# The first chunk of a Conformer block: rows and weights over two DMA queues, layer norm on VectorE, feed-forward matmuls tile by tile

## The chip, the cores and the metric

One core of one Trainium2 chip. The metric is the device time of one execution in microseconds (us); lower is better.

Engines: PE is TensorE (PEld its weight loads), DVE is VectorE, ACT is ScalarE, POOL is GpSimd, SP is SyncE, which only issues transfers here. "L506 PE MATMUL" is a matmul recorded at line 506 of the kernel.

## The reference, cut to what matters

```python
def reference(x, w_ff1_a, w_ff1_b, ...):       # x: 2 x 4000 x 512, bf16
    h = _layernorm(x, axis=-1)
    h = _silu(h @ w_ff1_a) @ w_ff1_b           # 512 -> 2048 -> 512
    x1 = x + 0.5 * h
    ...                                        # attention, convolution, a second feed-forward, layer norm
```

Tokens go through in 16 chunks of four tiles of 127. All that follows is about the first chunk's layer norm and the first four of its 16 feed-forward blocks (128 columns of `w_ff1_a` each). Weights and rows must arrive, be normalised and transposed before PE has real work: this is the head of the program.

## The kernel before

```python
# class Sync: every buffer remembers who wrote and read it; op() and dma() emit the waits
def dma(self, e, dkey, *fns, reads=(), writes=()):
    ...                                        # waits on engine e
    for fn in fns:
        fn(self.eng[e]).then_inc(self.sem[dkey], 16)
    ...

ROWS = ((0, 112), (112, TILE))                 # a tile of 127 rows is loaded in two pieces

def load_rows(self, dst, src, writes, eng):
    k = self.S.dsems[self.nxt("ld", 16)]
    return self.S.dma(eng, k, *[lambda e, lo=lo, hi=hi: e.dma_start(dst[lo:hi], src[lo:hi])
                                 for lo, hi in self.ROWS], writes=writes)

def ln_tiles(self, c, sl, prepare=None, engs=("ACT", "ACT", "ACT", "DVE"), src=None, lag=2):
    def finish(ti):
        if engs[ti] == "ACT":                  # -mean * factor, for ACT's scale and bias
            S.op("DVE", lambda e: e.scalar_tensor_tensor(out=self.sh[sl][:, ti:ti + 1], ...))
        self.ln_norm(c, sl, ti, self.ltm[ti][0:TILE, :], self.b_ltm[ti], engs[ti], src)
    for ti in range(TPC):
        ...
        self.ln_stats(c, sl, ti, src)          # bn_stats, DVE
        if ti >= lag:
            finish(ti - lag)
            yield ti - lag
        if lag == 1 or ti == TPC - 1:
            self.ln_mean(sl, ti)               # bn_aggr, DVE
            self.ln_factor(sl, ti)             # (var + eps) ** -0.5, POOL
    for ti in range(TPC - lag, TPC):
        finish(ti)
        yield ti

def head(self):
    self.warm(14)                              # 508-wide matmuls on zeros
    self.rings["ln"] = 1
    self.early = [self.sbank() for _ in range(4)]   # all four banks of the ring

    def blocks(lo, hi):                        # first layer, blocks 0 to 3, of tiles lo to hi - 1
        for f, (ps, b_ps) in enumerate(self.early):
            out = ps[:, lo * TILE:hi * TILE].rearrange("p (t k) -> p t k", t=hi - lo)
            for cc in range(DC):
                self.mm(out, self.Wa[:, cc, f * 128:(f + 1) * 128], self.lnT[0][:, lo:hi, cc, 0:TILE],
                        cc == 0, cc == DC - 1, [self.b_Wa[f * self.NWA // FC]] + self.b_lnT[0][lo:hi], b_ps)

    for ti in self.ln_tiles(0, 0, lag=1):
        if ti:                                 # four PE transposes, then a copy by ACT
            self.transpose_pe(ti - 1, 0, "ACT", (self.Yb[ti - 1], self.b_Y[ti - 1]))
        if ti == 2:
            blocks(0, 1)
    blocks(1, 2)
    self.transpose_pe(TPC - 1, 0, "DVE", (self.Yb[TPC - 1], self.b_Y[TPC - 1]))
    blocks(2, 4)

def program(self, any_score):
    ...
    for ti in range(TPC):
        self.load_rows(self.XT[ti], ..., [self.bx[ti]], "ACT" if ti == 1 else "SP")
    for k in range(self.NWA):                  # eight pieces of 256 KB of each weight
        self.load_wa(i["w_ff1_a"], k, "SP")
        self.load_wb(i["w_ff1_b"], 2 * k, 2 * k + 2)
        if k == 3:
            self.load_x(1)
    if not any_score:
        self.constants()                       # memsets on DVE and POOL
    self.act(self.nr1, self.onef, AF.Silu, ...)     # loads ACT's table early
    self.head()
    ...
```

`Wa0` and `Wa1` are the first two pieces of `w_ff1_a`: they hold blocks 0 to 3. `Wb0` is the first piece of `w_ff1_b`. After the head come the activations of the four early blocks and block 4, which uses the PSUM bank of block 0 again.

Of the kernel before, what the change touches and what calls it, by code (L numbers as in the profile page):

```python
# [15 lines left out]
TILE = 127  # L16
TPC = 4
# [10 lines left out]
DC = D // 128  # L28
FC = F // 128
# [51 lines left out]
class Sync:  # L81
# [103 lines left out]
        return None  # L185

    def dma(self, e, dkey, *fns, reads=(), writes=()):
        req = self._required(reads, writes)
        prev = self.count[dkey]
        if prev > 0:  # L190
            v = req.get(dkey)
            if v is None or v.val < prev:
                req[dkey] = Ev(dkey, prev, {})
        self._emit_waits(e, req)
        for fn in fns:
            fn(self.eng[e]).then_inc(self.sem[dkey], 16)
            self.count[dkey] += 16
        ev = Ev(dkey, self.count[dkey], dict(self.clock[e]))
        self._bind(ev, reads, writes)
        return ev  # L200

# [45 lines left out]
class Conformer:  # L247
# [315 lines left out]
        k = self.S.dsems[16 + self.nxt("tr", 12)]  # L563
        return self.S.dma("SP", k, lambda e: e.dma_start_transpose(dst, src), reads=reads, writes=writes)

    def load_rows(self, dst, src, writes, eng):
        k = self.S.dsems[self.nxt("ld", 16)]
        return self.S.dma(eng, k, *[lambda e, lo=lo, hi=hi: e.dma_start(dst[lo:hi], src[lo:hi])  # L568
                                     for lo, hi in self.ROWS], writes=writes)

    def store(self, dst, src, reads, writes):
        k = self.S.dsems[36 + self.nxt("st", 8)]
# [126 lines left out]

    def head(self):  # L700

        self.warm(14)
        self.rings["ln"] = 1
        self.early = [self.sbank() for _ in range(4)]

        def blocks(lo, hi):
            for f, (ps, b_ps) in enumerate(self.early):
                out = ps[:, lo * TILE:hi * TILE].rearrange("p (t k) -> p t k", t=hi - lo)
                for cc in range(DC):
                    self.mm(out, self.Wa[:, cc, f * 128:(f + 1) * 128], self.lnT[0][:, lo:hi, cc, 0:TILE],  # L710
                            cc == 0, cc == DC - 1, [self.b_Wa[f * self.NWA // FC]] + self.b_lnT[0][lo:hi], b_ps)

        for ti in self.ln_tiles(0, 0, lag=1):
            if ti:
                self.transpose_pe(ti - 1, 0, "ACT", (self.Yb[ti - 1], self.b_Y[ti - 1]))
            if ti == 2:
                blocks(0, 1)
        blocks(1, 2)
        self.transpose_pe(TPC - 1, 0, "DVE", (self.Yb[TPC - 1], self.b_Y[TPC - 1]))
        blocks(2, 4)  # L720

    def ln_mean(self, sl, ti):
        self.S.op("DVE", lambda e: e.bn_aggr(self.mv[sl][:, ti, :], self.st[sl][:, ti, :]),
# [616 lines left out]
    def program(self, any_score):  # L1340
        i = self.i
# [4 lines left out]
        self.scr = self.OT.rearrange("p c k -> p (c k)")[:, 0:512]  # L1346

        for ti in range(TPC):
            self.load_rows(self.XT[ti], self.x_flat[ti * TILE:(ti + 1) * TILE, :], [self.bx[ti]], "ACT" if ti == 1 else "SP")
        for k in range(self.NWA):  # L1350
            self.load_wa(i["w_ff1_a"], k, "SP")
            self.load_wb(i["w_ff1_b"], 2 * k, 2 * k + 2)
            if k == 3:
                self.load_x(1)
# [129 lines left out]
        for jj in range(DC):  # L1484
# [9 lines left out]
            else:  # L1494
                f, copy = self.depthwise(tail - 1, DC - 1)
# [131 lines left out]
```

## Time and profile before

| | before |
|---|---|
| time, median of the first three runs | 2045.01 us (2044.95 to 2045.12) |
| span of the profiled execution | 2040.1 us |
| PE busy | 2029.2 us, 98% of the chain that ended last |
| block 4 starts (PE runs without a stop after it) | 13.06 us |

The traced execution took 2043.9 us, about 1.1 us less than each of the timed ones, which have no trace.

The prediction reads the page, PE's timeline and the chain of the head. One view is added, VectorE's timeline in the head. Its columns are start, length, engine, line, operation, operands, count, and in brackets the idle time just before and what ended it.

```profile
7.15 0.16 DVE L676 SCALAR_TENSOR_TENSOR work<-work 127x1 f32<-127x1 f32 x1 [0.17 <-POOL work L728]
7.23 0.19 DVE L723 BATCH_NORM_AGGREGATE work<-work 127x2 f32<-127x9 f32 x1
8.15 0.41 DVE L638 TENSOR_SCALAR work<-xt,work 127x512 bf16<-127x512 bf16 x1 [0.74 <-POOL work L728]
```

This is the end of the layer norms: tile 2's shift for ScalarE, tile 3's aggregation, 0.74 us of waiting for GpSimd's power, and the only normalisation that VectorE does itself.

### The profile page before, as it was taken

How to read it: one execution, taken by the hardware profiler on the slowest of the kernel's cores; microseconds unless marked ns; L12 is line 12 of the kernel's file. 1: busy time of each engine (PE TensorE's matmuls, PEld its weight loads, DVE VectorE, ACT ScalarE, POOL GpSimd, SP SyncE). 2: the span in 40 equal slices, each digit the busy share in tenths (PEclk: the TensorE clock that was granted, in tenths of full speed). 3: DMA queues.
4: the chain of work that ended last, by engine and by line, in shares of the span. 5: the costliest groups of instructions: out<-in, count | busy, mean ns of one | idle time of the engine just before them, and what ended most of it. 6: DMA issues, size and time to landing. Idle time of an engine off the chain costs nothing.

```text
span 2040.1 us, 24550 instructions
## 1 busy us (share of the span) xinstructions
PE 2029.2 (99%) x9665; PEld 1029.8 (50%) x9667; DVE 1081.1 (53%) x2187; ACT 746.9 (37%) x1280; POOL 107.7 (5%) x235
## 2 busy tenths in 40 slices
PE   9999999999999999999999999999999999999998
PEld 5555555554444444445444444444455555555555
DVE  4234443334556667666766676667674444434433
ACT  3433333333333333333333333333345443443433
POOL 1000000000000000000000000000011000000000
PEclk9999999999999999999999999999999999999999
DMA  8222245320101111114421111111143111111111
GB/s 185 52 62 62 53 100 126 96 70 8 27 16 26 25 33 26 25 25 95 108 57 23 26 28 33 24 26 26 44 135 93 32 31 42 32 31 42 28 35 38
DMA packets 253122, 104.43 MB, mean 51 GB/s; under 512 B 193412, under 2 KB 252487, under 8 KB 252999
## 3 DMA queue, kind: packets, MB, share of 16 engines
q1 hardware_dynamic: 252751, 102.61, 20.9%
q8 instruction: 78, 1.28, 0.3%
q14 instruction: 45, 0.37, 0.1%
q10 hardware_dynamic: 248, 0.18, 0.0%
HBM read 33.77 MB, written 23.34 MB: 28 GB/s over the span
## 4 chain that ended last, share of the span: by engine, by line
PE 98%; DVE 1%; ACT 0%; DMA 0%; SPq 0%; POOL 0%; issue 0%; DVEq 0%; ACTq 0%
PE s L506 56%; PE y L506 42%; ACT work L556 0%; DVE wff L1206 0%; DMA wff<-in_w_ff_a_dram 0%; SPq L568 0%; POOL work L1215 0%; DVE work L553 0%; DVE wff L1100 0%; PE y L534 0%; ACT keys L556 0%; DVE work L1213 0%; SPq L560 0%; DVE work L869 0%; DVE work L952 0%
## 5 line engine op out<-in xcount | busy, mean ns | idle before, releaser
L556 ACT ACTIVATE work<-s 128x508 bf16<-128x508 f32 (+3 forms) x1060 | 622.7, 588 | 1211.8 <-PE s L506 1208.2
L506 PE MATMUL s<-work,wff 128*128 128x508 bf16 (+5 forms) x2624 | 628.3, 371 | 1.5 <-DVE work L553 0.8
L506 PE MATMUL s<-work,keys 128*128 128x508 bf16 (+1 forms) x2048 | 516.7, 374 | 0.1
L506 PE MATMUL y<-work,keys 128*128 128x508 bf16 (+2 forms) x2048 | 504.2, 373 | 0.4 <-DVE work L553 0.4
L506 PE MATMUL y<-wff,work 128*127 128x512 bf16 (+1 forms) x2000 | 501.4, 378 | 0.0
L952 DVE TENSOR_TENSOR work<-work 128x508 f32<-128x508 f32 (+2 forms) x496 | 334.6, 675 | 282.9 <-ACT work L556 281.8
L506 PEld LDWEIGHTS s<-work,wff 128*128 128x128 bf16 x2624 | 252.3, 98 | 278.0 <-issue 5.0
L506 PEld LDWEIGHTS y<-wff,work 128*127 128x127 bf16 x2000 | 274.4, 137 | 170.8
L506 PEld LDWEIGHTS s<-work,keys 128*128 128x128 bf16 x2048 | 199.4, 98 | 231.9 <-issue 0.6
L506 PEld LDWEIGHTS y<-work,keys 128*128 128x128 bf16 (+1 forms) x2048 | 193.5, 97 | 234.0 <-issue 6.2
L755 DVE SCALAR_TENSOR_TENSOR xt<-y,xt 127x512 bf16<-127x512 f32 x125 | 77.8, 684 | 364.9 <-PE y L506 364.9
L618 DVE BATCH_NORM_STATS2 work<-xt 127x6 f32<-127x512 bf16 x311 | 195.5, 678 | 4.8 <-DMA xt<-in_x_dram 4.7
L506 PE MATMUL s<-work 128*127 128x512 bf16 (+3 forms) x776 | 196.2, 377 | 1.6 <-DVE work L1324 1.2
L625 POOL TENSOR_TENSOR work<-work 127x4 f32<-127x4 f32 (+1 forms) x76 | 76.5, 1007 | 1130.4 <-DVE work L623 1130.4
L506 PEld LDWEIGHTS s<-work 128*127 128x127 bf16 (+1 forms) x776 | 94.7, 124 | 75.7 <-issue 2.7
L638 DVE TENSOR_SCALAR work<-xt,work 127x512 bf16<-127x512 bf16 x306 | 110.4, 407 | 27.0 <-POOL work L625 23.2
L755 DVE SCALAR_TENSOR_TENSOR xt<-s,xt 127x512 bf16<-127x512 f32 x55 | 38.0, 692 | 148.6 <-PE s L506 148.6
L755 DVE SCALAR_TENSOR_TENSOR xt<-s,work,xt 127x512 bf16<-127x512 f32 x64 | 48.0, 750 | 30.8 <-PE s L506 30.2
L1104 DVE SCALAR_TENSOR_TENSOR wff<-wff,s 128x508 bf16<-128x508 f32 (+1 forms) x57 | 38.7, 679 | 41.4 <-PE s L506 41.2
L556 ACT ACTIVATE wff<-s 128x508 f32<-128x508 f32 (+1 forms) x67 | 39.5, 591 | 54.6 <-PE s L506 54.6
L556 ACT ACTIVATE work<-keys,work 128x508 bf16<-128x508 bf16 (+1 forms) x68 | 52.3, 775 | 0.8 <-DVE work L1220 0.7
L1185 POOL COPY wff<-wff 128x1 bf16<-128x1 bf16 x56 | 10.4, 187 | 637.8 <-DVE wff L1104 635.0
(92 smaller groups left out, 415.7 us busy)
## 6 DMA issues: line engine op xcount, KB each, us to landing
keys<-keysd SPq DMA_DIRECT2D x62, 128.0 KB, 2.3
keysd<-work SPq DMA_DIRECT2D x14, 448.0 KB, 3.2
out_dram<-work SPq DMA_DIRECT2D x14, 448.0 KB, 3.2
dcvd<-wff SPq DMA_DIRECT2D x48, 127.0 KB, 1.8
keys<-dcvd SPq DMA_DIRECT2D x12, 508.0 KB, 5.4
xt<-in_x_dram SPq DMA_DIRECT2D x13, 448.0 KB, 4.7
wff<-in_w_ff_a_dram SPq DMA_DIRECT2D x16, 256.0 KB, 5.0
work<-work SPq DMA_TRANSPOSE x208, 2.5
```

Of the source, the lines that this page charges most:

```text
L506: self.S.op("PE", lambda e: e.matmul(out, lhsT, rhs, start=start, stop=stop, **kw), reads=reads, writes=[bank], inc=stop if inc is None el ...
L556: return self.S.op("ACT", lambda e: e.activation(out, in_, func, **kw), reads=reads, writes=writes)
L618: self.S.op("DVE", lambda e: e.bn_stats(self.st[sl][:, ti, 0:6], x), reads=[b_x], writes=[self.b_st[sl][ti]])
L625: S.op("POOL", lambda e: e.tensor_tensor(out=self.rs[sl][:, 0:n], in0=self.mv[sl][:, 0:n, 1], in1=self.neghalf[0:TILE, 0:n], op=ALU.pow), ...
L638: self.S.op("DVE", lambda e: e.tensor_scalar(out, x, self.mv[sl][:, ti, 0:1], self.rs[sl][:, ti:ti + 1], ALU.subtract, ALU.mult), reads=[b ...
L755: self.S.op("DVE", lambda e: e.scalar_tensor_tensor(out=self.XT[g][rows], in0=ps[rows], scalar=scalar, in1=self.XT[g][rows], op0=ALU.mult, ...
L952: S.op("DVE", lambda e, p=p, n=n, acc=acc: e.tensor_tensor(out=acc, in0=acc, in1=self.P[p][0:n, 0:W], op=ALU.add), reads=[self.b_P[p], sel ...
L1104: self.S.op("DVE", lambda e: e.scalar_tensor_tensor(out=out, in0=th, scalar=1.0, in1=ps[:, 0:W], op0=ALU.add, op1=ALU.mult), reads=[b_ps, ...
L1185: S.op("POOL", lambda e: e.tensor_copy(self.G[gs][:, jj, 0:1], self.G[gp][:, jj, CHUNK:CHUNK + 1]), reads=[self.b_G[gp][jj]], writes=[self ...
```

## The change

The intent is to have real work on PE sooner. The small row pieces of tiles 0 and 1, and the first two weights, go out on ScalarE's queue beside SP's; VectorE normalises all four tiles, which leaves ScalarE only the copies of transposes; each tile gets its own matmuls, so that tile 2's hide the copy of tile 3; one warm-up matmul (on zeros, to have PE's clock at its full rate when real work comes) goes.

```diff
@@ head @@
-        self.warm(14)
+        self.warm(13)
...
-        def blocks(lo, hi):
+        def blocks(ti):
             for f, (ps, b_ps) in enumerate(self.early):
-                out = ps[:, lo * TILE:hi * TILE].rearrange("p (t k) -> p t k", t=hi - lo)
                 for cc in range(DC):
-                    self.mm(out, self.Wa[:, cc, f * 128:(f + 1) * 128], self.lnT[0][:, lo:hi, cc, 0:TILE],
-                            cc == 0, cc == DC - 1, [self.b_Wa[f * self.NWA // FC]] + self.b_lnT[0][lo:hi], b_ps)
-
-        for ti in self.ln_tiles(0, 0, lag=1):
+                    self.mm(ps[:, ti * TILE:(ti + 1) * TILE], self.Wa[:, cc, f * 128:(f + 1) * 128],
+                            self.lnT[0][:, ti, cc, 0:TILE], cc == 0, cc == DC - 1,
+                            [self.b_Wa[f * self.NWA // FC], self.b_lnT[0][ti]], b_ps)
+
+        for ti in self.ln_tiles(0, 0, None, ("DVE",) * TPC, lag=1):
+            self.transpose_pe(ti, 0, "DVE" if ti == TPC - 1 else "ACT", (self.Yb[ti], self.b_Y[ti]))
             if ti:
-                self.transpose_pe(ti - 1, 0, "ACT", (self.Yb[ti - 1], self.b_Y[ti - 1]))
-            if ti == 2:
-                blocks(0, 1)
-        blocks(1, 2)
-        self.transpose_pe(TPC - 1, 0, "DVE", (self.Yb[TPC - 1], self.b_Y[TPC - 1]))
-        blocks(2, 4)
+                blocks(ti - 1)
+        blocks(TPC - 1)
@@ program @@
-            self.load_rows(self.XT[ti], ..., [self.bx[ti]], "ACT" if ti == 1 else "SP")
+            self.load_rows(self.XT[ti], ..., [self.bx[ti]], ("SP", "ACT" if ti < 2 else "SP"))
+        for k in range(2):
+            self.load_wa(i["w_ff1_a"], k, "ACT")
         for k in range(self.NWA):
-            self.load_wa(i["w_ff1_a"], k, "SP")
+            if k > 1:
+                self.load_wa(i["w_ff1_a"], k, "SP")
```

(A helper `dma_by` takes one engine for each piece.)

More of the change, by code (lines that the diff above doesn't have):

```diff
@@ L187, in dma, with dma_by @@
     def dma(self, e, dkey, *fns, reads=(), writes=()):
+        return self.dma_by((e,) * len(fns), dkey, *fns, reads=reads, writes=writes)
+    def dma_by(self, engs, dkey, *fns, reads=(), writes=()):
         req = self._required(reads, writes)
@@ L193, in dma @@
                 req[dkey] = Ev(dkey, prev, {})
-        self._emit_waits(e, req)
-        for fn in fns:
+        for e in dict.fromkeys(engs):
+            self._emit_waits(e, req)
+        for e, fn in zip(engs, fns):
             fn(self.eng[e]).then_inc(self.sem[dkey], 16)
             self.count[dkey] += 16
-        ev = Ev(dkey, self.count[dkey], dict(self.clock[e]))
+        snap = dict(self.clock[engs[0]]) if len(set(engs)) == 1 else {}
+        ev = Ev(dkey, self.count[dkey], snap)
         self._bind(ev, reads, writes)
@@ L564, in transpose, with load_rows @@
         return self.S.dma("SP", k, lambda e: e.dma_start_transpose(dst, src), reads=reads, writes=writes)
-    def load_rows(self, dst, src, writes, eng):
+    def load_rows(self, dst, src, writes, engs):
         k = self.S.dsems[self.nxt("ld", 16)]
-        return self.S.dma(eng, k, *[lambda e, lo=lo, hi=hi: e.dma_start(dst[lo:hi], src[lo:hi])
-                                     for lo, hi in self.ROWS], writes=writes)
+        return self.S.dma_by(engs, k, *[lambda e, lo=lo, hi=hi: e.dma_start(dst[lo:hi], src[lo:hi])
+                                                for lo, hi in self.ROWS], writes=writes)
     def store(self, dst, src, reads, writes):
@@ L1348, in program @@
         for ti in range(TPC):
-            self.load_rows(self.XT[ti], self.x_flat[ti * TILE:(ti + 1) * TILE, :], [self.bx[ti]], "ACT" if ti == 1 else "SP")
+            self.load_rows(self.XT[ti], self.x_flat[ti * TILE:(ti + 1) * TILE, :], [self.bx[ti]],
+                           ("SP", "ACT" if ti < 2 else "SP"))
+        for k in range(2):
+            self.load_wa(i["w_ff1_a"], k, "ACT")
         for k in range(self.NWA):
-            self.load_wa(i["w_ff1_a"], k, "SP")
+            if k > 1:
+                self.load_wa(i["w_ff1_a"], k, "SP")
             self.load_wb(i["w_ff1_b"], 2 * k, 2 * k + 2)
```

## The prediction

> **What bounds the kernel now.** I read the page first, then the waits of TensorE (PE) after the first chunk, then the start of the program: the timeline by engine, the chain of waits and the DMA landings.
>
> ```profile
> span 2040.1 us, 24550 instructions
> PE 2029.2 (99%) x9665; PEld 1029.8 (50%) x9667; DVE 1081.1 (53%) x2187; ACT 746.9 (37%) x1280; POOL 107.7 (5%) x235
> ...
> PE 98%; DVE 1%; ACT 0%; DMA 0%; SPq 0%; POOL 0%; issue 0%; DVEq 0%; ACTq 0%
> ```
>
> These are the page's head and its chain by engine. PE is busy for 2029.2 of 2040.1 us and carries 98% of the chain. The longest waits of PE after 39 us sum to 1.6 us (0.4, 0.4 and four of 0.2). So PE works through a fixed list, and any time won before its dense stretch moves everything after it forward by as much. No other stage is touched: set side by side without line numbers, the instruction orders of both kernels differ only in the head (and in its copy in the second, unused branch), but for one load on the SP queue (`w_o`) that now also waits for a weight landed long before. What counts is when PE becomes dense.
>
> The timeline of PE alone, from 5 us (start, length, operation, count, idle time before it and what ended that):
>
> ```profile
> 4.74 1.02 PE L506 MATMUL s<-work 128*128 128x508 bf16 x4
> 6.27 0.40 PE L521 MATMUL y<-work 127*128 127x127 bf16 x4 [0.51 <-ACT work L556]
> 7.21 0.40 PE L521 MATMUL y<-work 127*128 127x127 bf16 x4 [0.54 <-ACT work L556]
> 7.78 0.61 PE L506 MATMUL s<-work,wff 128*128 128x127 bf16 x8 [0.17 <-ACT work L556]
> 8.75 0.62 PE L506 MATMUL s<-work,wff 128*128 128x127 bf16 x8 [0.36 <-DMA wff<-in_w_ff_a_dram]
> 9.21 0.39 PE L521 MATMUL y<-work 127*128 127x127 bf16 x4
> 9.43 1.06 PE L506 MATMUL s<-work,wff 128*128 128x127 bf16 x16
> 10.33 0.39 PE L521 MATMUL y<-work 127*128 127x127 bf16 x4
> 11.33 2.77 PE L506 MATMUL s<-work,wff 128*128 128x254 bf16 x20 [0.61 <-DVE work L553]
> ```
>
> L521 are the transposes of tiles 0 to 3; the x8, x8 and x16 rows are the four first blocks for tile 0 and tile 1; the x20 row is 16 matmuls for tiles 2 and 3 together and 4 of block 4. After the last warm-up matmuls PE waits five times; from 11.33 it never stops. The 254-wide matmuls take about 0.108 us each (half of 0.216, the pitch of a 508-wide one: 4 in 0.866), so **block 4 starts at 11.33 + 16 x 0.108 = 13.06 us**. That moment is my yardstick. The chain over the first 14 us says why it is late:
>
> ```profile
> 3.89 0.51 SPq L560
> 4.40 0.04 issue
> 4.44 4.27 DMA wff<-in_w_ff_a_dram
> 8.71 0.05 issue
> 8.75 0.62 PE s L506 x8
> ```
>
> The second piece of the weights (Wa1) is issued only at 4.44, as the ninth transfer of the SP queue, lands at 8.71, and everything on PE queues behind it.
>
> **What the Trainium skill says.** "DMA: Bandwidth & Descriptors", section "Issuing engines are not separate DMA queues": transfers issued by several engines run on the same 16 DMA engines, and issuing from two saves only sequencer time. The trace has an issue at 0.33 to 0.51 us, so this is what the change can gain: 9 issues in a row on SP end near 4.4. The engines were half busy until 6 us (DMA share 0.50, 149 GB/s) and full from 6 to 8.75 (1.03, 295 GB/s), so issuing earlier does use idle time. "TensorE: Matmul & The Clock Gate", section "What's actually happening": half clock until some 3.4 us of sustained work, and half again after an idle window. The trace agrees with the first half: warm-up matmuls are 0.42 us apart until 4.10 and 0.216 after. "Perfetto Trace Analysis", section "Optimizing Scalar/DVE Operations": an instruction's reported length overlaps the next by its write acknowledgement. The trace agrees: a normalisation on VectorE lasts 0.41, four of them 1.38, so 0.325 each in a row. I use that pitch below.
>
> **The change part by part.**
>
> *Rows over two queues.* Tile 0's 15-row piece was issued at 1.18 and landed 2.3 us later, at 3.48; VectorE began its statistics at 3.47. Issued from ScalarE at 0.73, with the 2.4 us that this queue's pieces took, it lands at 3.13; the other piece at 0.73 + 2.2 = 2.93. VectorE's last memset ends at 3.21. So statistics start near 3.2, a gain of 0.27 us. The other tiles come earlier than needed.
>
> *First weights on ScalarE's queue.* Its two issues took 1.15 us together, so Wa0 goes out near 1.9 and Wa1 near 2.5 (before: 3.44 and 4.44). Wa0 took 2.8 us to land with the engines half busy; Wa1 behind it, sharing with tiles 2 and 3 and then Wb0, I estimate at 4 to 4.5: **6.5 to 7.0 instead of 8.71**. ScalarE's table load (1.28 us) slips to about 3.1 to 4.4, but its first real work comes at 5.8. SP's own weights (Wb1, Wa2, ...) also go out 1.06 us earlier.
>
> *All layer norm on VectorE.* Before, the period per tile was 1.00 us: aggregation at 4.20, power on GpSimd 4.48 to 5.03, a 0.16 us shift at 5.15, next aggregation at 5.22. Now the shift goes and the normalisation (pitch 0.325) stands between the power and the next aggregation. The lag from aggregation to normalisation is 0.92 (7.23 to 8.15 in the trace), so the period is about 0.94 + 0.325 = **1.26 us**. Aggregations: 3.93, 5.20, 6.46, 7.72; normalisations start 4.87, 6.13, 7.39, 8.64 and last 0.41. Tile 3 ends at 9.05, against 8.56 before: this part is slower for the last tile, but tile 0 (ended 6.16 on ScalarE) is now ready at 5.28.
>
> *Order on PE.* 13 warm-ups instead of 14 let go of PE near 5.4. A tile's four transposes occupy 0.22 us (9.21 to 9.43), results out 0.39 after their start; ScalarE's copy lasts 0.58, VectorE's 0.43, each with about 0.14 until PE starts; a tile's 16 matmuls take 0.90 (9.43 to 10.33); a normalisation reaches PE about 0.13 after its end. Step by step: T0 5.41; copy to 6.41. T1 6.67. Block 0 (needs T1 issued, copy 0, weights) 6.89 to 7.79, its Wa1 part at 7.34. T2 7.93; block 1 8.15 to 9.05. T3 9.18; copy on VectorE 9.60 to 10.03. Block 2 9.40 to 10.30 covers that copy, which before cost 0.61 idle. Block 3 10.30 to 11.20. The matmul work itself does not change: 64 x 0.056 = 3.6 against 32 x 0.056 + 16 x 0.108 = 3.5.
>
> *A new wait.* Block 4 uses the PSUM bank of the first early block again, so it needs that one's activation. Its last matmul is now only 12 before block 4: done at 10.30 + 4 x 0.056 + 0.20 = 10.73 (0.20 as 11.76 to 11.96 before), activation 0.59 to 11.32, 0.14 to PE: **block 4 at 11.46**, not 11.20.
>
> Sum: 13.06 - 11.46 = **1.6 us** earlier. After it PE needs Wa2 (before at about 10.3, now about 1 us earlier, needed at 11.46), Wb0 (before 7.0, needed 12.3), Wa3 (12.2, needed 14.9), Wa4 (16.3, needed 19.2): each has a margin, so nothing is given back. The next chunk's rows landed at 15.5 and are used after 37 us.
>
> **The rivals.**
>
> 1. *Weights stay late.* Two queues share the same full engines, and Wb0 may take turns with Wa1. If Wa1 lands at 8.0, its part of block 0 moves from 7.34 to 8.0 and all behind it by at most 0.5: gain 1.1, 2043.9. For: Wa1 took 4.27 in the old order. Against: it had Wa0 and Wb0 ahead of it on one queue, and an engine share of 0.50 before 6 us leaves room.
> 2. *VectorE becomes the bound.* If its period is 1.5 instead of 1.26, tile 3 comes 0.7 later; block 2 hides about 0.1 of it; gain near 1.0, 2044.0. For: normalisation and power now lie in series. Against: each of these durations is from the trace.
> 3. *PE's clock falls back* because one warm-up is gone, or work is thin from 5.4 to 6.7. Then 127-wide matmuls take 0.107 and about 3 us of work doubles: the gain is gone or negative, 2045 to 2047. Against: before, PE had gaps as wide and stayed at full pitch, and the new order is denser by 9 us.
> 4. *More than expected:* no wait for the bank, or PE reached earlier by the chain: at most 0.3 to 0.6 more, 2042.9.
>
> **Range and chances.** 2045.01 - 1.6 = 2043.4; I take 2043.5, as rivals 1 and 2 pull one way. The three times of before lie within 0.17 us, so noise hardly widens it: 2042.7 to 2044.3. Two per cent is 41 us and the whole head is 13, so the verdict must be the same: faster 0.003, same 0.99, slower 0.007.
>
> **What would show it.** Right: statistics of tile 0 near 3.2; normalisations on VectorE 1.26 apart, the last near 8.65; no wait of PE for weights, or below 0.3 us; PE's last idle time a short one (about 0.25) for ScalarE before block 4 near 11.5; the same list after it. Wrong: a weight's DMA in the chain after 7 us; warm-pitch lost (127-wide matmuls 0.1 us apart); block 4 after 12; or, with block 4 early, new DMA waits of PE between 12 and 25 us that give the time back.

## The result, and the profile after

| | before | after |
|---|---|---|
| time, median of four runs | 2045.07 us (2044.95 to 2045.14) | 2043.11 us (2042.81 to 2043.94) |
| span of the profiled execution | 2040.1 us | 2038.9 us |
| block 4 starts in it | 13.06 us | 11.87 us |

A ratio is the mean time of one kernel's fast runs over that of the other's fast runs of the same rounds, so not quite the ratio of the medians. Here it is 0.9991, 95% interval 0.9974 to 1.0008: the same at the 2% level, as forecast, and inside the predicted range (2042.7 to 2044.3).

The head of the page after:

```profile
span 2038.9 us, 24577 instructions
PE 2028.9 (100%) x9682; PEld 1030.0 (51%) x9682; DVE 1081.5 (53%) x2187; ACT 743.7 (36%) x1277; POOL 107.7 (5%) x235
```

PE has as much work as before (2028.9 against 2029.2 us) and a shorter span. In the kernel after, the same code stands a few lines later (L512 for L506). PE's timeline in the head:

```profile
5.42 0.39 PE L527 MATMUL y<-work 127*128 127x127 bf16 x4
6.64 0.40 PE L527 MATMUL y<-work 127*128 127x127 bf16 x4 [0.84 <-DVE work L644]
6.88 1.06 PE L512 MATMUL s<-work,wff 128*128 128x127 bf16 x16
8.34 0.40 PE L527 MATMUL y<-work 127*128 127x127 bf16 x4 [0.40 <-DVE work L644]
8.57 1.06 PE L512 MATMUL s<-work,wff 128*128 128x127 bf16 x16
9.59 0.40 PE L527 MATMUL y<-work 127*128 127x127 bf16 x4
9.82 3.08 PE L512 MATMUL s<-work,wff 128*128 128x127 bf16 x36
12.74 1.03 PE L512 MATMUL y<-wff,work 128*127 128x512 bf16 x4
```

The waits for ScalarE's normalisations and copies, for a weight and for VectorE's copy that the prediction showed are gone; two waits for normalisations are left. The x36 row is tiles 2 and 3 (32 matmuls) and block 4. Block 4 starts one block of 0.866 us before the second layer's first matmul: 12.74 - 0.87 = 11.87. The 32 matmuls issue in 1.79 us and are out at 11.61, so 0.26 us in between is the wait for block 0's activation.

Up to 6.88 each entry is within 0.03 us of the prediction (5.41, 6.67, 6.89). The transposes of tile 2 are 0.41 late (7.93 predicted, 8.34 measured), and that delay remains to the end. VectorE's timeline and the chain of waits say why:

```profile
5.35 0.65 DVE L624 BATCH_NORM_STATS2 work<-xt 127x6 f32<-127x512 bf16 x1
...
7.27 0.70 DVE L624 BATCH_NORM_STATS2 work<-xt 127x6 f32<-127x512 bf16 x1 [0.58 <-DMA xt<-in_x_dram]
7.88 0.40 DVE L644 TENSOR_SCALAR work<-xt,work 127x512 bf16<-127x512 bf16 x1
...
9.12 0.41 DVE L644 TENSOR_SCALAR work<-xt,work 127x512 bf16<-127x512 bf16 x1 [0.73 <-POOL work L731]
```

```profile
3.01 4.24 DMA xt<-in_x_dram
7.25 0.02 issue
7.27 0.10 DVE work L624
```

Statistics of tile 3 start at 7.27 (at 6.61 where its rows are in time, below), because the tile's last 15 rows, issued at 3.01, land only at 7.25. VectorE takes its instructions in order, so tile 2's normalisation, whose power GpSimd had ready at 7.32, stands behind them and starts at 7.88 instead of the predicted 7.39. The same small piece in the DMA view (last figure: us from issue to landing), first before, then after:

```profile
xt<-in_x_dram SPq DMA_DIRECT2D x1, 15.0 KB, 1.9
```

```profile
xt<-in_x_dram SPq DMA_DIRECT2D x1, 15.0 KB, 4.2
```

And what the engines carried after the change from 4.0 to 5.4 us (queue: packets, MB, share of the 16 engines' time; q10 is ScalarE's queue, q1 SP's):

```profile
q10 hardware_dynamic: 720, 0.36, 86.4%
q1 hardware_dynamic: 100, 0.08, 20.5%
```

The weights of the new queue have most of the engines while SP's last rows wait.

**The accounting.** In 11 of the 14 traces PE's last matmul ends 2021.49 to 2021.53 us after the start of block 4; in the others it is 2021.64, 2021.69 and 2022.02. So what the head wins is kept, as far as PE goes. From there to the end of the span it is 5.1 to 6.4 us in the same instructions: the final store's 112 KB took 3.2 us from issue to landing in the first trace of before and 4.0 in the second. One time is therefore no measure of the head to better than a microsecond. **The start of block 4 is the yardstick below**, and times stand beside it.

### The profile page after: what moved, and what is told of

Same layout as the page of the kernel before. It is cut to its first block, busy times and chain, and to the rows that moved or that the text cites. A ratio compares the mean times of both kernels' runs of the same rounds, so it can differ in the third digit from the quotient of the medians.

```text
span 2038.9 us, 24577 instructions
## 1 busy us (share of the span) xinstructions
PE 2028.9 (100%) x9682; PEld 1030.0 (51%) x9682; DVE 1081.5 (53%) x2187; ACT 743.7 (36%) x1277; POOL 107.7 (5%) x235
## 4 chain that ended last, share of the span: by engine, by line
PE 98%; DVE 1%; ACT 0%; DMA 0%; issue 0%; POOL 0%; SPq 0%; DVEq 0%; ACTq 0%
PE s L512 56%; PE y L512 42%; ACT work L562 0%; DVE wff L1209 0%; DMA xt<-in_x_dram 0%; POOL work L1218 0%; SPq L574 0%; DVE wff L1103 0%; PE y L540 0%; ACT keys L562 0%; DVE work L559 0%; DVE work L1216 0%; PE y L527 0%; DVE work L872 0%; DVE work L955 0%
## 5 line engine op out<-in xcount | busy, mean ns | idle before, releaser
L512 PE MATMUL s<-work,wff 128*128 128x508 bf16 (+4 forms) x2640 | 628.4, 369 | 0.4 <-DVE work L559 0.2
L512 PE MATMUL s<-work 128*127 128x512 bf16 (+4 forms) x775 | 196.0, 377 | 1.6 <-DVE work L1327 1.2
L512 PEld LDWEIGHTS s<-work 128*127 128x127 bf16 (+2 forms) x775 | 94.6, 124 | 75.6 <-issue 2.7
```

The source lines that it names most:

```text
L512: self.S.op("PE", lambda e: e.matmul(out, lhsT, rhs, start=start, stop=stop, **kw), reads=reads, writes=[bank], inc=stop if inc is None el ...
```

## The experiments

All twelve runs gave correct results. Kernels are compared only within the same rounds. All ratios have intervals of about ±0.0014, so none differs from 1 by its time alone.

| run | block 4, us | median, us | ratio to before |
|---|---|---|---|
| before again | 12.73 | 2044.40 | 0.9998 |
| after again | 11.93 | 2042.91 | 0.9993 |
| after, all rows first, both weights on ACT's queue | 13.42 | 2046.40 | 1.0008 |
| after, both weights on SP again | 12.95 | 2043.74 | 0.9995 |
| after, tiles 2 and 3 in one group | 12.63 | 2043.63 | 0.9994 |
| before, the weights on ACT's queue alone | 13.26 | 2044.94 | 1.0001 |
| after, tiles 0 to 2 normalised on ACT | 13.43 | 2044.69 | 0.9999 |
| after, rows first, one weight on each queue | 11.68 | 2043.42 | 0.9993 |
| after, rows first, all weights on SP | 11.43 | 2042.79 | 0.9994 |
| after, 10 warm-ups | 11.85 | 2042.72 | 0.9993 |
| rows first, weights on SP, 10 warm-ups | 11.43 | 2042.39 | 0.9991 |
| the same, a memset moved behind the head | 11.12 | 2042.25 | 0.9991 |

The theory: tile 3's late rows set the end of the head after the change, and they are late because the weights went to a second queue. The rival: the series of layer norms on VectorE sets it, whatever the rows do.

### Controls: both kernels again

No edit.

> Control: the kernel before, unchanged. Its first trace belongs to an execution of 2043.9 us, while its timed runs gave 2044.95 to 2045.14. Theory 1 (that execution was a lucky one and the head varies): a trace of this run may show block 4 later than 13.06 us, up to 14.1. Theory 2 (the head is fixed, the difference lies elsewhere): block 4 at 13.06 again. Time 2045.0, equal to before within 0.05%.

> Control: the kernel after, unchanged, to see how far its own time spreads (its first four runs: 2042.81 to 2043.94). Theory that the spread comes from how the two queues' packets interleave, and so from when the rows of tile 3 land: the time spreads by about 1 us again, block 4 between 11.5 and 13. Rival, a spread of the chip and not of the kernel: the kernel before, run beside it, spreads as much. Mean 2043.2.

Measured: block 4 at 12.73 and 11.93; mean times 2044.26 for before again, 2043.18 for after again, 2044.67 for the nine runs of before beside them. Neither theory of the first text held: block 4 came earlier (Wa1 had landed before PE needed it), not later, and not at the same place. The spread of after (2042.64 to 2043.99) is no wider than that of before (2043.74 to 2045.25), so the rival fits: no spread of the change's own shows. The traces differ at another place. The warm-ups of the first trace after, then of the second (PE's timelines):

```profile
3.69 1.89 PE L512 MATMUL s<-work 128*128 128x508 bf16 x7
```

```profile
3.69 2.96 PE L512 MATMUL s<-work 128*128 128x508 bf16 x7
```

The same seven matmuls last 1.1 us longer in the second, as PE's clock was lifted later. There tile 0's transposes waited for the warm-ups (6.49 instead of 5.42), and still block 4 came only 0.06 later: tile 3 was late as well, with statistics at 7.32.

### All rows first, both weights on ScalarE's queue

```diff
-                           ("SP", "ACT" if ti < 2 else "SP"))
+                           ("SP", "ACT"))
```

> The kernel after, but all four tiles' large row pieces go first on SP and all four small ones on ScalarE's queue, then the two weights on ScalarE's queue. Theory (the weights of the second queue delay the rows of tile 3, which sets the end of the head): tile 3 lands before 5.5 us instead of 7.25, its statistics start near 6.6, block 4 at about 11.5 if Wa1 lands before 7.3; Wa1 is now issued near 3.3 and may land near 7.5 to 8, then block 4 near 11.8; time 2042.6 to 2043.1, with less spread. Rival (VectorE's series of normalisations sets it, not the rows): block 4 stays at 11.9 whatever the rows do.

```profile
9.57 0.62 PE L512 MATMUL s<-work,wff 128*128 128x127 bf16 x8 [1.90 <-DMA wff<-in_w_ff_a_dram]
```

A miss, and a useful one. The rows were in time (tile 3's statistics at 6.62, the last normalisation at 8.69, which the prediction had at 8.64), but Wa1, issued at 3.15, landed 6.4 us later at 9.5, since SP's queue, done with the rows, now sent Wb0, Wb1 and Wa2 beside it. PE waited 1.90 us for it. This trace is of the fastest of the five executions (2044.01); the others took 2044.46 to 2047.83, and where they lost more is not known. Two queues delay each other: in after it was the rows, here the weight.

### Both weights on SP again

```diff
         for k in range(2):
-            self.load_wa(i["w_ff1_a"], k, "ACT")
         for k in range(self.NWA):
-            if k > 1:
-                self.load_wa(i["w_ff1_a"], k, "SP")
+            self.load_wa(i["w_ff1_a"], k, "SP")
```

(The emptied loop is dropped.)

> The kernel after, but the first two weights are issued on SP after the rows, as in the kernel before; rows over two queues, layer norm on VectorE and single-tile blocks stay. Theory: tile 3 lands near 4.9 and its statistics start at 6.6, but Wa1 lands at 8.7 as before, PE waits for it from 7.3, and block 4 starts near 12.6 (0.7 later than after, 0.45 earlier than before): time about 2043.8. Rival (the weights' queue does not matter, only the layer norm's order does): block 4 at 11.5 to 11.9, time 2043 or less.

```profile
9.10 0.62 PE L512 MATMUL s<-work,wff 128*128 128x127 bf16 x8 [1.00 <-DMA wff<-in_w_ff_a_dram]
```

Tile 3 was in time: its last rows, on the same queue and issued at 3.01 as in after, landed at 4.86 instead of 7.25, so it is the weights on the other queue that delay them. Its statistics started at 6.61. But Wa1 came at 9.05 and block 4 at 12.95, 1.08 later than after. The theory's direction holds; 12.6 was expected, as Wa1 had landed at 8.71 in the first trace. So the second queue for the weights does earn its place in this order of issue, rows late or not.

### Tiles 2 and 3 in one group of matmuls

```diff
-        def blocks(ti):
+        def blocks(lo, hi):                # as in the kernel before
...
-            if ti:
-                blocks(ti - 1)
-        blocks(TPC - 1)
+            if ti in (1, 2):
+                blocks(ti - 1, ti)
+        blocks(2, 4)
```

> The kernel after, but the blocks of tiles 2 and 3 are again one group of 254-wide matmuls, as in the kernel before. Theory (single-tile blocks hide the last tile's copy): PE again stands idle about 0.6 us for VectorE's copy of tile 3; the copy ends near 10.5, 16 matmuls of 0.108 follow, block 4 near 12.35, without the short wait for ScalarE before it: 0.45 us later than after. Rival (the copy was not what cost, the wait for the bank takes its place in full): block 4 within 0.15 of 11.9.

```profile
10.89 2.77 PE L512 MATMUL s<-work,wff 128*128 128x254 bf16 x20 [0.61 <-DVE work L559]
```

The idle 0.61 us is back and the bank's wait gone; block 4 at 12.63, 0.76 later than after. Of that, 0.3 is not the grouping: tile 3's statistics started at 7.56 in this execution, against 7.27. The rest, about 0.45, is what was expected.

### The weights on ScalarE's queue alone, in the kernel before

```diff
+        for k in range(2):
+            self.load_wa(i["w_ff1_a"], k, "ACT")
         for k in range(self.NWA):
-            self.load_wa(i["w_ff1_a"], k, "SP")
+            if k > 1:
+                self.load_wa(i["w_ff1_a"], k, "SP")
```

> The kernel before, with one part of the change alone: the first two weights on ScalarE's queue. Theory (the second queue takes the DMA engines from the rows of tile 3): no wait of PE for weights any more, but tile 3's rows land near 7.2, the last statistics start near 7.3, and with them shift, normalisation and transposes of tiles 2 and 3 come later: block 4 at 13.1 to 13.3, no gain over before (12.7 to 13.1), time 2044.5 to 2045. Rival (earlier weights are the gain by themselves): block 4 near 12.4.

VectorE's timeline, then ScalarE's:

```profile
7.48 0.69 DVE L618 BATCH_NORM_STATS2 work<-xt 127x6 f32<-127x512 bf16 x1 [0.68 <-DMA xt<-in_x_dram]
```

```profile
8.27 0.81 ACT L556 ACTIVATE work<-xt,work 127x512 bf16<-127x512 bf16 x1 [0.15 <-DVE work L676]
```

As expected: PE waits for no weight, but tile 3's rows are late, with them tile 2's shift and its normalisation on ScalarE (8.27), and block 4 comes at 13.26, no earlier than in either trace of before. The last piece of tile 3's rows landed at 7.46 (4.85 before). PE's clock was late too (14 warm-ups, until 7.26), but the chain that ended last does not pass through it: it goes from these rows over shift, normalisation and tile 1's copy to PE at 9.62. The part that removes the wait named in the chain gains nothing by itself.

### Layer norm of tiles 0 to 2 on ScalarE

```diff
-        for ti in self.ln_tiles(0, 0, None, ("DVE",) * TPC, lag=1):
+        for ti in self.ln_tiles(0, 0, None, ("ACT", "ACT", "ACT", "DVE"), lag=1):
```

> The kernel after, with tiles 0 to 2 normalised on ScalarE as before (VectorE computes the shift), tile 3 on VectorE; all else stays. Theory: ScalarE now alternates normalisations (0.80 each) with copies (0.58), in series: transposes at about 6.1, 8.0, 9.9, then tile 3, block 4 near 13.2; so the move to VectorE is worth about 1.3 us in this order. Rival (the rows of tile 3 set the end in any case): block 4 below 12.3.

```profile
8.25 0.40 PE L527 MATMUL y<-work 127*128 127x127 bf16 x4 [1.39 <-ACT work L562]
```

Block 4 at 13.43, 1.56 later than after, where 1.3 was expected. Not all of it is the layer norm's: the chain that ended last begins with the warm-ups, which a late clock stretched to 6.64 in this execution.

```profile
1.18 5.46 PE s L512 x13
```

Tile 0's normalisation had ended on ScalarE at 6.00, so its transposes, at 6.47, came about 0.3 late. An estimate from these figures is that VectorE's part is worth about 1.2 us in this order of emission. ScalarE does normalisation, copy, normalisation, copy in series, and tile 1's transposes start 1.6 us later than after.

### Rows first, one weight on each queue

```diff
-                           ("SP", "ACT" if ti < 2 else "SP"))
-        for k in range(2):
-            self.load_wa(i["w_ff1_a"], k, "ACT")
+                           ("SP", "ACT"))
+        self.load_wa(i["w_ff1_a"], 0, "SP")
+        self.load_wa(i["w_ff1_a"], 1, "ACT")
```

> The kernel after with all rows first (large pieces on SP, small ones on ScalarE's queue), then Wa0 on SP and Wa1 on ScalarE's queue, then the other weights on SP. The run with rows first and both weights on ScalarE's queue had tile 3 in time but Wa1 at 9.5, as SP's later weights took half the engines. Theory (it is bytes ahead of a transfer over both queues that count): Wa0 and Wa1 each have half the engines and land at 6.2 to 7.2, no wait for them, tile 3's statistics at 6.6; block 4 at 11.5 if PE's clock is lifted early (4 us), 11.9 if late (6 us, where 13 warm-ups last until 6.6). Time 2042.5 to 2043.1. Rival (ScalarE's queue is served worse in any case): Wa1 lands after 8, block 4 after 12.

```profile
7.83 0.62 PE L512 MATMUL s<-work,wff 128*128 128x127 bf16 x8 [0.23 <-DMA wff<-in_w_ff_a_dram]
```

Block 4 at 11.68: the rows were in time and Wa1 0.23 us late. It landed at 7.79, 5.1 us after its issue at 2.71; 7.2 at the latest was expected, and no wait. The rival's figures (Wa1 after 8, block 4 after 12) were not reached, and in after ScalarE's queue carried more than SP's (0.36 against 0.08 MB from 4.0 to 5.4 us), so it is not served worse in any case. In this execution 0.5 us was lost later in PE's list (2022.02 instead of 2021.5), 0.3 of it in one wait for a transposing transfer between 500 and 1000 us. Whether that is chance was not tried.

### Rows first, all weights on SP

```diff
-                           ("SP", "ACT" if ti < 2 else "SP"))
+                           ("SP", "ACT"))
         for k in range(2):
-            self.load_wa(i["w_ff1_a"], k, "ACT")
+            self.load_wa(i["w_ff1_a"], k, "SP")
```

> The kernel after with all rows first (large pieces on SP, small ones on ScalarE's queue) and then all weights on SP alone, Wa0 and Wa1 ahead of Wb0. Theory (a transfer waits for the bytes ahead of it in its own queue and for what the other queue puts beside it): behind the rows Wa0 and Wa1 have the engines to themselves and land near 5.7 and 6.8; rows of tile 3 before 5.5; no wait of PE for a DMA; block 4 at 11.45 if the clock is lifted before 5.5 us, 11.9 if later. Rival (two queues carry more in sum, so one queue alone is slower): Wa1 after 7.5, block 4 after 11.7.

VectorE's timeline and PE's:

```profile
6.61 0.65 DVE L624 BATCH_NORM_STATS2 work<-xt 127x6 f32<-127x512 bf16 x1
...
8.68 0.41 DVE L644 TENSOR_SCALAR work<-xt,work 127x512 bf16<-127x512 bf16 x1 [0.73 <-POOL work L731]
```

```profile
9.38 3.08 PE L512 MATMUL s<-work,wff 128*128 128x127 bf16 x36
```

This settles the theory against its rival. With the rows in time and the rest of the change as it was, block 4 starts at **11.43**, 0.44 earlier than after. Wa1 landed 3.4 us after its issue, against 6.4 and 5.1 in the two runs above, where the other queue had bytes beside it. It is not always 3.4: in the two runs with this order and 10 warm-ups below it took 4.3 and 3.8, and the 4.3 (landing at 7.30) was just in time for PE. The chain of waits of this head names VectorE, GpSimd and PE, and no transfer.

### Fewer warm-ups, and an earlier start

```diff
-        self.warm(13)
+        self.warm(10)
```

> The kernel after with 10 warm-up matmuls instead of 13. All at half clock they end at 1.17 + 10 x 0.427 = 5.44, so tile 0's transposes can start at 5.4 in every run, where 13 end at 5.4 to 6.7 (by when the clock is lifted, 4.1 to 7.1 in the traces so far). Theory (tile 3's rows set the end of this head): nothing gained, block 4 at 11.9 again. Rival (late warm-ups cost time in the untraced runs): mean time 0.2 to 0.4 lower and less spread. Risk: the clock is lifted later, the 127-wide matmuls start at half rate, block 4 after 12.3.

> All rows first, all weights on SP alone, and 10 warm-ups. Theory: with rows and weights in time and PE free at 5.44, the series of VectorE and the bank's wait alone remain: block 4 at 11.45 whenever the clock is lifted before 7; time 2042.6. If the clock comes later because PE idles, block 4 at 12 or later.

> As the run before it, and the 0.27 us memset that VectorE does just before tile 0's statistics comes after the head. Theory (VectorE's series of layer norms sets the end once rows and weights are in time): statistics of tile 0 start near 3.0 instead of 3.24, every normalisation 0.2 earlier, block 4 near 11.25. Rival (PE's own list is the bound): block 4 stays at 11.45.

The third also moves one line of `constants()` behind `self.head()`:

```diff
-        S.op("DVE", lambda e: e.memset(self.XT[SHARED][HALF - 32:HALF], 0.0), writes=[self.bx[SHARED]])
```

Ten warm-ups alone: 11.85, nothing gained, as the theory has it (tile 3's statistics at 7.25 again). Whether the untraced executions gained, the rival, stays open: after with 13 warm-ups was not run in this call. With rows and weights in time: 11.43, as with 13 in a run of early clock; the clock was not lost in any of the three traces. With the memset behind the head VectorE begins sooner:

```profile
2.93 0.69 DVE L624 BATCH_NORM_STATS2 work<-xt 127x6 f32<-127x512 bf16 x1
```

Its 0.31 us go straight through: block 4 at 11.12. So once transfers are in time, VectorE's series is the bound; it now starts as soon as tile 0's rows, landed at 2.90, allow. This is the version with the earliest block 4 and the lowest median: 2042.25 us, 2042.12 to 2042.42, ratio 0.9991, against 2043.81 of before.

## Why the prediction was right, point by point

- **What bounds the kernel: right.** PE's list after block 4 is rigid; its length is the same to 0.04 us in 11 of 14 traces, through changes of the head of over 2 us.
- **VectorE's series: right.** Statistics of tile 0 at 3.24 (3.2 predicted). With rows in time the last normalisation starts at 8.68 (8.64), so the period of 1.26 holds. (The working takes 0.94 from aggregation to normalisation where its own line gives 0.92; 0.93 was measured.)
- **Weights: right.** Wa1 landed at 6.89 (6.5 to 7.0 predicted), and PE no longer waits for them. Undoing that part costs 1.08 us; doing it alone gains nothing.
- **The new wait for block 0's bank: right**, 0.26 predicted and 0.26 measured.
- **The rows: the step that failed** is "The other tiles come earlier than needed." Tile 3 landed at 7.25 instead of the 4.85 of before, about 0.65 after it was needed, for the sharing that the prediction counted against Wa1 only. This cost 0.41 us: block 4 moved by 1.19 us and not by 1.6, and the last normalisation began at 9.12, not near 8.65. Where the rows were kept ahead of the weights, block 4 came at 11.43, against 11.46 in the working. Rival 1 had the right mechanism, turned upon the other queue.
- **The clock: right**, no 127-wide matmul at half rate in either trace of after; with 10 warm-ups block 4 came no later either. The trace read in the prediction had 2.9 us of work (1.17 to 4.10) before the fast pitch, where the text cites 3.4.
- **The time: close in part by luck.** 2043.5 was predicted and 2043.11 measured, although the head won 0.41 us less than predicted. The forecast subtracted a gain read in an execution of 2043.9 us from the 2045.01 of other executions. Between the traced executions themselves the difference is 1.0 (2043.9 and 2042.88), which fits the head's 1.19. The means of the timed executions differ by 1.8 us in the first comparison and by 1.5 in the second, where block 4 moved by only 0.80 between the traces and the time from PE's last matmul to the end was 1.0 shorter. The timed runs have no traces, so whether the final store or later heads of before make up the rest stays open.

## What to carry to other kernels

In this kernel a second DMA queue saved issue time and changed what landed first: tile 3's last rows came at 7.25 us instead of 4.85. Put what is needed first ahead in one queue, and use a second queue only for issue time, with small pieces. After removing a wait, ask which transfer's bytes have been pushed back, and whether an in-order engine has ready work behind it; and when a head is a few microseconds, measure it by a fixed event in the trace, as the end of the program varies by as much.

## What the Trainium skill lacked or had wrong

- "DMA: Bandwidth & Descriptors", section "Issuing engines are not separate DMA queues", says that transfers of several engines interleave and that issuing from several only saves issue time. The runs show that it also reorders what lands: 15 KB of rows took 4.2 us instead of 1.9 with weights on the other queue, and 256 KB of weights 6.4 with later weights beside them, 3.4 to 4.3 behind the rows in one queue.
- The same page, section "Queues, rings and completion order", has each engine take turns between queues packet by packet, but not what shares come of it. From 4.0 to 5.4 us the trace of after counts 720 packets (0.36 MB) of ScalarE's queue and 100 (0.08 MB) of SP's, while the latter's rows were still due until 7.25. A packet of the page holds several descriptors and need not be one of the trace's records, so this does not refute even turns; why the shares are so uneven is not known from the runs.
- "TensorE: Matmul & The Clock Gate", section "What you observe", has the clock rise around 4 us into the work, ±500 ns from run to run. Here the first matmul starts at 1.17 us, and the clock records in the 14 traces (not in the views shown) rise to the full rate between 3.9 us (rows first, all weights on SP) and 7.1 us (weights on ScalarE's queue alone, all 14 warm-ups 0.42 apart): 2.7 to 5.9 us into the work. The page's own remark that the window runs free fits this better: the stretch at full clock is 2030.93 or 2034.34 us long in all 14 traces, 3.41 apart, whichever the kernel.
- No page has how far one store varies between executions of a program: the last 112 KB took 2.8 to 4.0 us from issue to landing in the traces, which limits what one time can tell.
